# Visits of two chunks from chunk 8, seven tiles of transposed keys and queries, and new rows of operations, in a retention and squared-ReLU kernel

## The chip, the cores and the metric

One core of a Trainium2 chip. The metric is the device time of one execution in microseconds (us), median of the runs shown.

## The reference, cut to what matters

```python
# retention: q, k, v are (4, 8, 768, 64); gamma = 1 - 2**(-5 - h) for head h
for t in range(S):
    state = gamma * state + einsum('bhd,bhe->bhde', k[:, :, t], v[:, :, t])
    y[:, :, t] = scale * einsum('bhd,bhde->bhe', q[:, :, t], state)
x = y.transpose(0, 2, 1, 3).reshape(3072, 512)
h = maximum(x @ w_in, 0)          # w_in 512 x 2048
out = (h * h) @ w_out             # w_out 2048 x 512
```

## The kernel before, in words

The 3072 tokens are 24 chunks of 128, six for each of four sequences. Work is recorded as named operations, and for each engine a row of names (`TURNS`, L280 to L344) fixes by hand in which order that engine takes them. Every engine is in order: an operation that waits holds up all that stand behind it in its row. SP's row holds nearly all DMAs, ACT's some stores.

The names, with the number of a chunk or a block behind them:

- `ldq`, `ldk`, `ldv` (L694): loads of one chunk of q, k, v, 256 KB each, from SP, into one of four slots each. Chunks 0 to 3 are loaded in pairs (L529). `ldwin`, `ldwout` (L946): loads of the weights into the staging tiles `wst`; a `ldwout` and the last two `ldwin` are 1 MB.
- `cq`, `ck`, `cv`, `cwin`, `cwout`: casts of what was loaded to bf16 (L510 to L514, L704), each a quarter of a weight piece or one chunk.
- `X` (L736): the DMA transpose of the cast keys and queries of a chunk from 7 on into one of `NQT` tiles `qkT`. Chunks 4 and 5 are transposed by TensorE (`T`, `E`), chunk 6 inside visit V.5 (`E6`).
- `V m.n` (`visit`, L801): TensorE's work of a visit. It ends chunk m (values, and queries times states, into `yy`) and begins chunk n (scores and sums of keys and values, into `sc`). `U`/`V m-m.n-n` (`visit2`, L865) does that for two chunks at a time, its sums in two PSUM banks of the shared four. `P`, `S`, `Y` on VectorE mask the scores, add up the state, and scale the output into `xt`.
- `F1.b.f` (`ffn1`, L971): eight matmuls of block b of tokens with w_in; `R` (ReLU, ACT, L978) and `Q` (square, ACT or VectorE, L990 and L992) follow, through two tiles `r`.
- `F2` (L1149): the second product for chunks 0 to 3, in quarters of w_out, with `O` on ACT. `M1` to `M7` (`products`, L1079): for every later pair of chunks the second product as seven products in place of eight, with sums of weights `WT`, sums of activations `H`, and the evictions `e`, `u`, `v`, `ca`, `cb`, `cc`, `cd`.
- `st`: stores of the output.

Which form a visit has is decided by this loop (`DOUBLE` is 10, `SPLIT` is 6, `NPAIR` is 2):

```python
if n >= DOUBLE:
    if n % 2 == 0:
        visit2([x for x in (n - 2, n - 1) if n > DOUBLE or x == n - 1], [x for x in (n, n + 1) if x < NM])
elif n < 2 * NPAIR:
    ...
else:
    visit(m, n if n < NM else None, t)
```

So the visits of before are V.4, V4., V.5, V5.6, V6.7, V7.8, V8.9, V9.10-11, V10-11.12-13 and so on to V22-23. TensorE's row mixes them with groups F1, F2 and M of about 0.87 us each. A class `Plan` gives the operations their PSUM banks and tiles and puts all rows in one sequence.

Of the kernel before, what the change touches and what calls it, by code (L numbers as in the profile page):

```python
# [18 lines left out]
class Plan:  # L19
# [47 lines left out]
    def schedule(self, nbanks, max_open, nslots):  # L67
# [176 lines left out]
BLOCKS = [2, 2, 1, 1, 2, 2, 2, 2, 2, 2, 2, 2, 2]  # L244
SPLIT = 6
AHEAD = 4
DOUBLE = 10
WARM = 20.0
FILL = 0.215
WARMING = 18.4  # L250
# [28 lines left out]

TURNS = {  # L280
    "POOL": (
        "iota3 ident iota iota2 cmask2 cmask ck0.0 cq0.1 cv0.0 cv0.1 ck2.1 cv2.0 cwin1.0 cwin1.2 cq4 cwin3.2 "
        "cwin4.1 cwin5.2 cwin5.0 cwout0.3 cwout0.2 cwout1.1 cwout1.2 cwout1.3 cwout2.0 cq6 cq5 cwout3.3 cwout3.2 "
        "cq7 ck8 cq8 ck10 cq11 ck11 v.4 v.6 cq13 ck14 cq19 ck16 cq16 cq17 ck17 ck18 cq20 ck20 ck21 ck23 v.12 v.16 "
        "v.18 v.20 "
    ),
    "DVE": (
        "lng lnt ex2_f ex_f vf2 vf Ek0.0 Ek0.1 Eq0.0 P0.10 P0.01 P0.00 P0.11 S1 cq2.1 Y0.0 Y0.1 Ek2.1 P2.01 P2.00 "
        "cv2.1 cwin0.2 P2.10 S2 P2.11 cwin2.0 Y2.0 S3 Y2.1 Q0.2 cwin3.0 Eq4 cwin4.3 ck4 Q1.0 cv4 Q1.2 Ek4 Q1.10 "
        "S4.0 P4 cwin5.1 Y4 Q0.10 ck5 Q0.14 S4.1 cwout0.1 cwout1.0 WT1.0 WT1.1 cwout2.3 WT3.0 Q1.12 WT2.0 WT2.1 "  # L290
# [12 lines left out]
    "ACT": (
        "vf20 vf0 yf0 yf1 yf2 yf3 ck0.1 cq0.0 Eq0.1 cq2.0 S0 Eq2.0 ck2.0 Ek2.0 Eq2.1 cwin0.0 R0.0 cwin2.2 Q0.0 "
        "R0.2 R0.4 Q0.4 R1.0 R1.4 Q1.4 cwin4.0 cwin4.2 R1.2 R0.6 Q0.6 R1.10 R1.6 cwin5.3 Q1.6 R0.8 Q0.8 R1.8 "
        "R0.10 cwout0.0 Q1.8 R0.14 R2.4 Q2.4 R0.12 R2.12 Q0.12 R2.8 Q2.8 cwout2.2 R1.12 cwout2.1 Q2.12 R2.0 Eq5 "
        "cwout3.1 cwout3.0 Ek5 ck6 R1.14 Q2.0 O0 E6 O1 R3.8 O3 O2 R3.0 cq10 Q3.0 Q3.8 R3.12 R3.4 Q3.4 R4.4 Q4.4 "
        "R4.12 Q4.12 R4.10 R4.0 Q4.0 Q4.10 R4.6 e.4 R4.8 Q4.8 Q4.6 R4.2 Q4.2 R4.14 Q4.14 ca.4 ck12 e.6 R5.10 "
        "R5.14 cq12 R5.0 R5.4 Q5.4 R5.2 st4.0 Q5.2 R5.8 R5.6 ca.6 Q5.8 R5.12 Q5.12 st4.1 e.8 st6.1 ca.8 R6.0 R6.8 "
        "Q6.0 Q6.8 R6.4 R6.10 Q6.10 R6.12 R6.2 Q6.2 R6.6 R6.14 R7.4 Q7.4 R7.12 R7.2 Q7.2 R7.14 Q7.14 R7.6 R7.10 "  # L310
        "Q7.10 e.10 R7.0 Q7.0 st8.0 R7.8 Q7.8 Q7.6 ca.10 R8.0 R8.8 Q8.0 R8.6 Q8.8 R8.14 Q8.6 R8.10 R8.2 Q8.10 "
        "R8.4 Q8.4 R8.12 Q8.12 st10.1 e.12 R9.0 R9.2 cq21 R9.8 Q9.2 R9.4 Q9.4 st10.0 ca.12 R9.10 R9.12 Q9.8 ck22 "
        "R9.6 st12.1 R9.14 Q9.6 e.14 Q9.14 cq23 R10.8 Q10.8 R10.10 R10.6 R10.0 ca.14 R10.4 Q10.0 R10.14 Q10.14 "
        "R10.2 R10.12 Q10.2 R11.12 e.16 R11.4 R11.8 Q11.8 R11.6 R11.2 R11.10 Q11.10 R11.0 R11.14 Q11.14 ca.16 "
# [12 lines left out]
        "Tk0.0 Tk0.1 Tq0.1 Tq0.0 A0.1 A0.0 B0 B1 Tq2.0 C0.0 C0.1 Tk2.0 Tk2.1 Tq2.1 A2.0 A2.1 B2 B3 F1.0.0 C2.0 "
        "C2.1 F1.0.2 F1.0.4 F1.1.0 F1.1.4 Tq4 F1.1.2 F1.0.6 F1.1.6 Tk4 F1.1.10 F1.0.10 V.4 F1.0.8 F1.1.8 V4. "
        "F1.0.12 F1.0.14 F1.2.4 F1.2.12 F1.2.0 F1.2.8 F1.1.12 F2.1.0 F2.0.0 F2.0.1 F2.1.1 Tq5 F2.1.2 Tk5 F1.1.14 "
        "F2.0.2 F2.1.3 F2.0.3 V.5 F2.2.0 F2.2.1 F2.3.0 F2.3.1 V5.6 F2.2.2 F2.3.2 F2.3.3 F1.3.8 V6.7 F2.2.3 M1.4 "  # L330
        "F1.3.0 F1.3.12 V7.8 F1.3.4 F1.4.4 F1.4.10 F1.4.12 F1.4.0 M5.4 F1.4.6 F1.4.8 F1.4.2 M6.4 V8.9 F1.4.14 "
        "M2.4 M3.4 M7.4 M1.6 M5.6 M4.4 U9.10-11 V9.10-11 M2.6 F1.5.10 F1.5.14 F1.5.0 F1.5.4 F1.5.2 F1.5.8 M6.6 "
        "F1.5.6 M3.6 F1.5.12 M7.6 M1.8 M4.6 M5.8 U10-11.12-13 V10-11.12-13 M2.8 M6.8 M3.8 F1.6.0 F1.6.8 M7.8 "
        "F1.6.4 F1.6.10 U12-13.14-15 V12-13.14-15 M4.8 F1.6.12 F1.6.2 F1.6.6 F1.6.14 F1.7.4 F1.7.14 F1.7.12 "
        "F1.7.2 F1.7.6 M1.10 F1.7.10 M5.10 F1.7.0 U14-15.16-17 V14-15.16-17 F1.7.8 M2.10 M3.10 F1.8.0 F1.8.8 "
        "M6.10 F1.8.6 F1.8.14 M7.10 F1.8.10 F1.8.2 M4.10 F1.8.4 U16-17.18-19 V16-17.18-19 F1.8.12 M1.12 M5.12 "
        "F1.9.0 F1.9.2 F1.9.8 F1.9.4 M2.12 M6.12 M3.12 F1.9.10 M7.12 F1.9.12 F1.9.6 M4.12 U18-19.20-21 "
        "V18-19.20-21 F1.9.14 M1.14 M5.14 M6.14 F1.10.8 F1.10.10 M2.14 F1.10.6 M3.14 F1.10.0 F1.10.4 M7.14 "
        "F1.10.14 U20-21.22-23 V20-21.22-23 F1.10.2 M4.14 F1.10.12 M1.16 F1.11.12 F1.11.4 M5.16 F1.11.8 M6.16 "
        "V22-23. F1.11.6 M2.16 F1.11.2 F1.11.10 M7.16 F1.11.0 F1.11.14 M3.16 F1.12.2 M4.16 F1.12.8 F1.12.6 "  # L340
        "F1.12.10 F1.12.4 F1.12.0 F1.12.12 M1.18 M5.18 F1.12.14 M6.18 M2.18 M3.18 M7.18 M1.20 M5.20 M4.18 M6.20 "
        "M2.20 M3.20 M7.20 M1.22 M5.22 M4.20 M6.22 M2.22 M7.22 M3.22 M4.22 "
    ),
}  # L344

# [2 lines left out]
def kernel(  # L348
# [29 lines left out]
    blk0 = [sum(blocks[:i]) for i in range(NB)]  # L378
    for x, n in zip(blk0, blocks):
        assert 512 % (n * C) == 0 and x // 4 == (x + n - 1) // 4  # L380
    NLD, NBF, NQT, NXT, NH2, NWS, NOSB, NST = 4, 5, 5, 3, 3, 4, 3, 6
    NR, NUN = 2, 2
    NBANK = 4

# [3 lines left out]
    def sb(name, shape, dt):  # L388
        return const.tile(shape, dt, name=name)

    ident = sb("ident", [P, P], BF16)
    cmask = sb("cmask", [P, L], BF16)
# [12 lines left out]
    cmask2 = sb("cmask2", [P, 2, C], BF16)  # L405
# [773 lines left out]
    for m in range(-1, NM):  # L1179
        n = m + 1  # L1180
        if n > DOUBLE:
            xs = range(prepared, min(NM, n + AHEAD) if n % 2 else prepared)
# [6 lines left out]
        t = m + 2 if NPE <= m + 2 < NTD else None  # L1189
# [65 lines left out]
```

## Time and profile before

| | us |
|---|---|
| runs, median of 3 (lowest to highest) | 207.31 (206.76 to 207.9) |
| profiled execution, its own time | 207.57 |
| its span, first to last instruction | 205.8 |
| busy: PE, DVE, ACT, POOL | 192.9, 144.5, 121.1, 37.3 |
| HBM read, written | 27.26 MB, 6.29 MB |

Busy times come from one profiled execution, whose own time stands 0.26 us above the median. PE is TensorE's matmuls, PEld its weight loads, DVE VectorE, POOL GpSimd, SP the engine whose queue issues DMAs. In the timeline of an engine, square brackets tell of idle time before an instruction and of what ended it. The chain of waits is followed back from the last instruction; "issue" is a wait for nothing that the profile shows. Matmul ends are modelled and overlap, so steps from start to start are used for PE. The landing of a load is the time at which its semaphore is complete, issue plus time to landing in the view of the DMA issues.

### The profile page before, as it was taken

The numbers are of one execution on the slowest core, as the hardware profiler recorded it, in microseconds if no ns is written. First come the engines' busy times: TensorE is split into PE (matmuls) and PEld (weight loads), VectorE is DVE, ScalarE is ACT, GpSimd is POOL, SyncE is SP. The second block draws the span as 40 slices with busy tenths as digits, with TensorE's granted clock in tenths as the row PEclk, the third lists the DMA queues.
The fourth block names the chain that finished last, engine by engine and source line by source line (L and its number), as shares of the span: only waits on it lengthen the run. The fifth ranks groups of instructions, "written<-read, shape, count | busy, mean of one in ns | idle before, by whom it ended". The sixth has DMA issues, their size and how long they took to land.

```text
span 205.8 us, 7031 instructions
## 1 busy us (share of the span) xinstructions
PE 192.9 (94%) x3030; PEld 160.7 (78%) x3034; DVE 144.5 (70%) x287; ACT 121.1 (59%) x216; POOL 37.3 (18%) x62
## 2 busy tenths in 40 slices
PE   8988999969799999998899999989999999999993
PEld 6655888744479788887788898878888988888882
DVE  2586687554764978869778978796778797576332
ACT  8463699679037992771357977666575555764110
POOL 6532314451300132001114012113000020001100
PEclk9996999999999999999999999999999999999999
DMA  5999999999999999999999999999961100020222
GB/s 163 290 317 320 291 316 358 300 272 204 217 205 250 172 243 160 231 234 250 182 187 204 147 268 189 221 227 195 160 171 58 45 12 3 27 76 3 104 102 102
DMA packets 95503, 38.46 MB, mean 187 GB/s; under 512 B 81008, under 2 KB 89456, under 8 KB 95472
## 3 DMA queue, kind: packets, MB, share of 16 engines
q1 hardware_dynamic: 93744, 35.00, 81.2%
q10 hardware_dynamic: 1728, 3.02, 4.3%
q8 instruction: 23, 0.38, 0.8%
q14 instruction: 8, 0.07, 0.1%
HBM read 27.26 MB, written 6.29 MB: 163 GB/s over the span
## 4 chain that ended last, share of the span: by engine, by line
PE 59%; DMA 18%; SPq 16%; POOL 2%; issue 2%; DVE 1%; ACT 1%; ACTq 0%; POOLq 0%
PE fps L971 28%; PE fps L1079 27%; DMA kn<-in_k_dram 8%; SPq L694 7%; SPq L946 5%; DMA wst<-in_moe_w_out_dram 5%; DMA qkT<-kqs 5%; SPq L529 2%; SPq L736 2%; PE sc L786 1%; POOL w_out L514 1%; PE yy L760 1%; PE yy L775 1%; PE fps L798 1%; DVE h L992 1%
## 5 line engine op out<-in xcount | busy, mean ns | idle before, releaser
L971 PE MATMUL fps<-xt,w_in 128*128 128x256 bf16 (+1 forms) x832 | 92.3, 266 | 0.9 <-ACT w_in L510 0.5
L971 PEld LDWEIGHTS <-w_in 128*128 128x128 bf16 x832 | 75.5, 98 | 9.9 <-ACT w_in L510 0.6
L978 ACT ACTIVATE r<-fps 128x512 f32<-128x512 f32 x96 | 55.8, 592 | 41.6 <-PE fps L971 37.1
L990 ACT ACTIVATE h<-r 128x512 bf16<-128x512 f32 x60 | 37.1, 626 | 1.1
L1079 PEld LDWEIGHTS <-h 128*128 128x128 bf16 x320 | 31.0, 98 | 5.7 <-issue 1.8
L992 DVE TENSOR_TENSOR h<-r 128x512 bf16<-128x512 f32 x36 | 26.2, 732 | 8.6 <-ACT r L978 8.1
L1079 PEld LDWEIGHTS <-wst 128*128 128x128 bf16 x240 | 23.5, 98 | 3.8 <-issue 1.0
L1079 PE MATMUL fps<-w_out,h 128*128 128x256 bf16 x160 | 20.9, 273 | 0.7 <-issue 0.7
L1079 PE MATMUL fps<-wst,h 128*128 128x256 bf16 x160 | 20.7, 273 | 0.6 <-DVE wu L1102 0.6
L1079 PE MATMUL fps<-wst,wst 128*128 128x256 bf16 x160 | 20.6, 272 | 0.0
L514 POOL CAST kqs<-kn 128x512 bf16<-128x512 f32 x10 | 7.2, 718 | 47.3 <-DMA kn<-in_k_dram 23.5
L704 DVE TENSOR_TENSOR vs<-vn,vf 128x512 bf16<-128x512 f32 x20 | 13.6, 686 | 3.0 <-DMA vn<-in_v_dram 3.0
L1149 PE MATMUL fps<-w_out,h 128*128 128x512 bf16 x60 | 14.2, 379 | 0.5 <-issue 0.5
L514 POOL CAST kqs<-qn 128x512 bf16<-128x512 f32 x11 | 7.8, 706 | 26.8 <-DMA qn<-in_q_dram 11.5
L1105 ACT ACTIVATE wst<-fps 128x512 f32<-128x512 f32 x10 | 5.9, 592 | 10.9 <-PE fps L1079 10.9
L919 DVE TENSOR_TENSOR state<-fps,state 128x256 bf16<-128x256 f32 x23 | 9.7, 420 | 3.2 <-PE yy L775 2.7
L1113 ACT ACTIVATE osb<-fps 128x256 f32<-128x256 f32 x10 | 3.8, 381 | 13.6 <-PE fps L1079 13.5
L927 DVE TENSOR_TENSOR xt<-yy,yf 128x512 bf16<-128x512 f32 x15 | 10.0, 682 | 2.3 <-PE yy L775 2.3
L1079 PE MATMUL fps<-w_out,wst 128*128 128x256 bf16 x80 | 10.5, 272 | 0.8 <-issue 0.8
L1149 PEld LDWEIGHTS <-h 128*128 128x128 bf16 x64 | 6.0, 98 | 6.4 <-issue 0.2
L1102 DVE TENSOR_TENSOR osb<-fps,wst 128x256 f32<-128x256 f32 x15 | 6.3, 420 | 6.2 <-PE fps L1079 2.9
L775 PE MATMUL yy<-qkT,state 64*64 64x64 bf16 x296 | 8.4, 195 | 1.1 <-DVE state L851 1.0
(99 smaller groups left out, 208.7 us busy)
## 6 DMA issues: line engine op xcount, KB each, us to landing
qn<-in_q_dram SPq DMA_DIRECT2D x20, 256.0 KB, 5.5
kn<-in_k_dram SPq DMA_DIRECT2D x20, 256.0 KB, 5.5
vn<-in_v_dram SPq DMA_DIRECT2D x20, 256.0 KB, 5.8
wst<-in_moe_w_out_dram SPq DMA_DIRECT2D x4, 1024.0 KB, 9.7
out_dram<-osb SPq DMA_DIRECT2D x10, 256.0 KB, 4.3
out_dram<-osb ACTq DMA_DIRECT2D x9, 256.0 KB, 3.1
wst<-in_moe_w_in_dram SPq DMA_DIRECT2D x4, 512.0 KB, 8.5
wst<-in_moe_w_in_dram SPq DMA_DIRECT2D x2, 1024.0 KB, 8.5
```

Source lines behind the costliest of these rows:

```text
L514: nc.gpsimd.tensor_copy(o, t)
L694: lambda x=x, t=t: nc.sync.dma_start(t.rearrange("s (h d) -> s h d", h=H), src[x][b, :, i * C : (i + 1) * C, :].rearrange("h s d -> s h d")))
L704: lambda: nc.vector.tensor_tensor(out=o[:], in0=t.rearrange("s (h d) -> s h d", h=H), in1=vf[:, i, :, None].to_broadcast([P, H, D]), op=AL ...
L775: nc.tensor.matmul(yy[L * c : L * c + L, sub, 256 * x + p * L : 256 * x + p * L + L], lhsT=st[r, j, :], rhs=qkT[r, 1, j, sub * L : sub * L ...
L927: lambda xt=xt, u=u, i=i, x=x: nc.vector.tensor_tensor(out=xt[:, :, u * C : u * C + C].rearrange("s p (g t) -> s g p t", g=2), in0=yy[:, : ...
L946: lambda: nc.sync.dma_start(st, wv))
L971: nc.tensor.matmul(ps[:, u * n : u * n + n], lhsT=w_in_bf[j][:, cb, c * P : (c + 1) * P], rhs=xt[:, cb, cols], start=(cb == 0), stop=(cb = ...
L978: nc.scalar.activation(o, t, AF.Relu)
L990: nc.scalar.activation(hv, rv, AF.Square)
L992: (nc.vector if on == "DVE" else nc.gpsimd).tensor_tensor(out=hv, in0=rv, in1=rv, op=ALU.mult)
L1079: nc.tensor.matmul(ps[:, 256 * half : 256 * half + 256], lhsT=a[left][:, f], rhs=right(f), start=(first and f == 0), stop=True, skip_group ...
L1149: nc.tensor.matmul(ps[:, 0:w], lhsT=h2[:, fb, u * C : u * C + C], rhs=w_out_bf[j][:, c, ns], start=(fb == 0), stop=(fb == NFB - 1))
```

## The change

`DOUBLE` goes from 10 to 8, so chunks 8 and 9 are begun and ended in visits of two: V7.8-9, V8-9.10-11, V10-11.12-13 in place of V7.8, V8.9, V9.10-11, V10-11.12-13. `NQT` goes from 5 to 7 tiles `qkT`. The rows of all five engines are other ones, with the same operations; some move to another engine (casts, squares, stores).

```diff
-DOUBLE = 10
+DOUBLE = 8
...
-    NLD, NBF, NQT, NXT, NH2, NWS, NOSB, NST = 4, 5, 5, 3, 3, 4, 3, 6
+    NLD, NBF, NQT, NXT, NH2, NWS, NOSB, NST = 4, 5, 7, 3, 3, 4, 3, 6
```

SP's row up to X15, then TensorE's row up to V10-11.12-13, before and after (the rows run on in the same manner):

```diff
-ldk0 ldq0 ldv0 ldq2 ldk2 ldv2 ldwin0 ldwin1 ldwin2 ldq4 ldwin3 ldwin4 ldk4 ldv4 ldwin5 ldwout0 ldk5
-ldwout1 ldwout2 ldq6 ldq5 ldwout3 ldk6 ldv5 ldk7 ldq7 ldv6 ldk8 ldq8 ldv7 X7 ldv8 st0 ldq10 X8 ldq9 ldk9
-ldv9 ldk10 st3 st2 ldk11 ldq11 X9 ldv10 ldv11 X10 ldk12 X11 ldq13 ldv12 st1 ldq12 ldq14 ldk13 ldv13
-ldk15 ldq15 ldk14 X12 X13 ldq19 ldv14 X14 ldv15 X15
+ldk0 ldq0 ldv0 ldq2 ldk2 ldv2 ldwin0 ldwin1 ldwin2 ldq4 ldwin3 ldwin4 ldk4 ldv4 ldwout0 ldq5 ldq6 ldwin5
+ldv5 ldk5 ldwout1 ldq7 ldk6 ldwout3 ldwout2 ldk7 ldv6 ldk9 ldq9 ldk8 ldq8 ldv7 X7 ldv9 ldv8 X9 X8 st0
+ldq11 ldk12 ldq10 ldk10 ldk11 ldv10 ldq13 st2 st3 ldq12 ldv11 X10 ldk13 X11 st1 X12 ldv12 ldv13 X13
+ldq15 ldq14 ldk15 ldk14 st6.0 ldq17 ldv14 ldv15 X15 ldv16 X14
...
-Tk0.0 Tk0.1 Tq0.1 Tq0.0 A0.1 A0.0 B0 B1 Tq2.0 C0.0 C0.1 Tk2.0 Tk2.1 Tq2.1 A2.0 A2.1 B2 B3 F1.0.0 C2.0
-C2.1 F1.0.2 F1.0.4 F1.1.0 F1.1.4 Tq4 F1.1.2 F1.0.6 F1.1.6 Tk4 F1.1.10 F1.0.10 V.4 F1.0.8 F1.1.8 V4.
-F1.0.12 F1.0.14 F1.2.4 F1.2.12 F1.2.0 F1.2.8 F1.1.12 F2.1.0 F2.0.0 F2.0.1 F2.1.1 Tq5 F2.1.2 Tk5 F1.1.14
-F2.0.2 F2.1.3 F2.0.3 V.5 F2.2.0 F2.2.1 F2.3.0 F2.3.1 V5.6 F2.2.2 F2.3.2 F2.3.3 F1.3.8 V6.7 F2.2.3 M1.4
-F1.3.0 F1.3.12 V7.8 F1.3.4 F1.4.4 F1.4.10 F1.4.12 F1.4.0 M5.4 F1.4.6 F1.4.8 F1.4.2 M6.4 V8.9 F1.4.14
-M2.4 M3.4 M7.4 M1.6 M5.6 M4.4 U9.10-11 V9.10-11 M2.6 F1.5.10 F1.5.14 F1.5.0 F1.5.4 F1.5.2 F1.5.8 M6.6
-F1.5.6 M3.6 F1.5.12 M7.6 M1.8 M4.6 M5.8 U10-11.12-13 V10-11.12-13
+Tk0.0 Tk0.1 Tq0.1 Tq0.0 A0.1 A0.0 B0 B1 Tq2.0 C0.0 C0.1 Tk2.0 Tk2.1 Tq2.1 A2.0 A2.1 F1.0.0 B2 F1.0.2 B3
+C2.0 C2.1 Tq4 F1.0.4 F1.1.4 F1.1.2 F1.1.6 F1.1.0 Tk4 F1.0.6 V.4 F1.1.8 F1.1.10 V4. F1.0.10 F1.0.8 F1.2.0
+F1.2.4 F1.2.8 Tq5 F1.0.12 F1.1.14 F1.0.14 F1.2.12 F1.1.12 Tk5 F2.0.0 F2.1.0 V.5 F2.1.1 F2.0.1 F2.0.2
+F2.0.3 F2.1.2 F2.2.0 F2.1.3 V5.6 F2.2.1 F2.2.2 F1.3.4 F1.3.12 F1.3.0 V6.7 F2.2.3 F2.3.0 F2.3.1 F2.3.2
+F2.3.3 U7.8-9 V7.8-9 F1.3.8 F1.4.4 F1.4.12 F1.4.10 F1.4.6 M1.4 F1.4.2 F1.4.0 M5.4 F1.4.14 F1.4.8 M6.4
+M2.4 M3.4 M7.4 M1.6 M5.6 M4.4 U8-9.10-11 V8-9.10-11 M2.6 M6.6 M3.6 F1.5.2 F1.5.12 F1.5.14 M7.6 F1.5.0
+U10-11.12-13 V10-11.12-13
```

ACT's row of after has, around the casts of w_out, `cwout1.3 Q0.14 cwout3.3 cwout2.1 cwout2.2 cwout3.0 ck7 R1.12 Q2.12 E6 O0`. SP's row between X15 and X19 gains, ahead of X17, the loads ldq18 and ldv18, and ahead of X18 the loads ldk20, ldk21, ldq21 and ldq22.

## The prediction

> **What bounds the kernel now.** I read the page, then the busy times by window, the waits and timeline of PE, and the chain of waits. The page first:
>
> ```profile
> PE 192.9 (94%) x3030; PEld 160.7 (78%) x3034; DVE 144.5 (70%) x287; ACT 121.1 (59%) x216; POOL 37.3 (18%) x62
> DMA  5999999999999999999999999999961100020222
> q1 hardware_dynamic: 93744, 35.00, 81.2%
> ```
>
> PE is busy for 94% of the span, yet the 16 DMA engines are full too, from the start to slice 29, about 150 us. Nearly all of it is one queue, SP's, and what stands late in SP's row lands late. By window (us, PE, PEld, DVE, ACT, POOL, granted clock, DMA share, GB/s):
>
> ```profile
> 15.00:20.00 5.00, 3.85 (x64) 2.29 (x62) 3.46 (x8) 1.23 (x3) 1.17 (x2) 0.74 1.14 319
> 20.00:25.00 5.00, 4.85 (x69) 4.15 (x66) 2.99 (x6) 3.35 (x7) 1.23 (x2) 0.91 1.15 325
> 40.00:45.00 5.00, 3.37 (x19) 1.51 (x18) 3.10 (x5) 3.33 (x6) 2.34 (x3) 1.00 0.86 244
> 95.00:100.00 5.00, 3.95 (x152) 3.38 (x152) 4.97 (x12) 0.60 (x1) 0.00 (x0) 1.00 1.23 144
> 170.00:175.00 5.00, 5.00 (x48) 4.47 (x47) 3.77 (x8) 2.95 (x5) 0.00 (x0) 1.00 0.01 3
> ```
>
> PE has holes at 40 to 45 and 95 to 100, and none near the end. The timeline of PE says what ended the larger ones:
>
> ```profile
> 43.98 0.40 PE L745 MATMUL fps<-ident,kqs 128*128 128x128 bf16 x4 [1.63 <-POOL kqs L514]
> 54.42 0.25 PE L775 MATMUL yy<-qkT,state 64*64 64x64 bf16 x6 [0.97 <-DVE state L851]
> 93.13 1.03 PE L1079 MATMUL fps<-wst,h 128*128 128x256 bf16 x8 [0.62 <-DVE wu L1102]
> 99.73 0.49 PE L1079 MATMUL fps<-w_out,wst 128*128 128x256 bf16 x3 [0.85 <-issue]
> ```
>
> The first is Tq5 behind cq5 behind ldq5, a load that stands late in SP's row. The chain of waits shows the same queue further on:
>
> ```profile
> 27.07 10.15 DMA wst<-in_moe_w_out_dram
> 49.09 4.68 DMA kn<-in_k_dram
> 91.98 3.85 DMA qkT<-kqs
> 99.41 5.94 DMA qkT<-kqs
> 105.39 0.32 PE sc L786 x16
> ```
>
> The transposes X13 and X15 land at 95.83 and 105.35, and the scores of their visits start 0.04 us later. After 105.4 the chain is almost PE alone. So up to about 105 us the SP queue is level with PE, and afterwards PE sets the end.
>
> **The change part by part.** *Visits.* V7.8, V8.9, V9.10-11 and V10-11.12-13 become V7.8-9, V8-9.10-11 and V10-11.12-13. From start to next start the undisturbed ones before took 0.66 and 0.73 (one chunk each way) and 1.16 to 1.22 us (two). V7.8-9 and V9.10-11 lie between; I take 1.0. The sum goes from 0.66+0.73+1.0+1.2 to 1.0+1.2+1.2: 0.2 to 0.3 us of PE saved.
>
> *Seven tiles.* They let a transpose land before the visit that reads its predecessor is over. Before, the X transposes wait for casts or simply queue: X15 reuses chunk 10's tile, which is free at 96.6, and is issued at 99.41 behind ldv15. So more tiles release nothing that waits; worth 0, except that pairs at chunk 8 would need them.
>
> *New rows: which loads come when.* This decides. Cost per entry from landings before (issue plus time to landing): from ldv4 (27.35) to ldwout3 (45.88) five 1 MB weights and three 256 KB loads took 18.53; to ldv7 (55.92) eight loads took 10.04, that is 1.25 each; to X11 (80.38) eleven loads, three stores and about 4.5 transposes took 24.46. With stores 0.75 (most of their steps are 0.69 to 0.76) and a load 1.2 this gives 2.0 for a transpose, half of it behind its landing, and 3.0 for a weight. Undisturbed loads step by 1.05, undisturbed weights by 2.87; these are the lower bounds.
>
> (a) Weights. Up to ldv4 SP's row is the same. Then ldwout2 comes last of the weights, behind five weights (its own included) and six loads in place of three: 27.35+5x3.0+6x1.2 = 49.5 (48.0 at the lower bounds; before, the last weight landed at 45.88). ACT casts two of its quarters one after the other, 0.63 each: ready at 50.8. PE gets to F2.0.2, which reads it, much sooner. In the new row F1.0.0 still starts near 17.5; then come B2, F1.0.2, B3, C2.0, C2.1 and Tq4, so F1.0.4 starts about 22.95 (before 22.10, without Tq4). Five F1 groups at 0.874 to 27.3, Tk4, F1.0.6 and V.4 to 28.9, two groups and V4. to 31.3, five groups and Tq5 to 35.9, one us for ldwin5's casts, five groups to 41.3, Tk5, two F2 groups of 0.87, V.5 (0.66), two more F2: 45.7. PE then stands for 5 us; nothing else in its row may pass.
>
> (b) After it: five F2 groups to 55.1, V5.6 (0.8) to 55.9, five groups to 60.3, V6.7 to 61.0, five to 65.4. V7.8-9 wants X8 and X9. Counting from before's X9 (73.20), four loads and three stores are no longer ahead of X8, the later one: 73.20-4.8-2.3 = 66.1; counted forward from ldwout2 it is 65.3. I take 65.7, the visit ends at 66.4. Before, V5.6 was through at 55.17 with 150 matmul groups (F1, F2, M) left; now 55.9 with 153. That is 3.3 us behind.
>
> (c) Eighteen groups (15.7) bring PE to 82.2. X11 has three more loads ahead: 80.38+3.6 = 84.0, or 83.5 counted forward. V8-9.10-11 ends at 84.4, 0.7 after X11, as V10-11.12-13 and V12-13.14-15 did after X13 and X15. X13 has four loads fewer ahead, 91.0, and does not hold V10-11.12-13 (91.8). Fourteen groups later V12-13.14-15 meets X14 at 105.5 to 106.6 (before X15 105.35; two loads and a store more, a load and a store fewer) and ends at 106.7.
>
> (d) Fifteen groups: 119.9. X17 has two loads more ahead: 118.86+2.4 = 121.2, or 120.7. V14-15.16-17 ends at 121.7 with 88 groups left. Before it ended at 119.57, also with 88 left. X18, with four loads more and a store fewer ahead, lands at 133.2, when PE comes to V16-17.18-19; X21 (146.5) is early, and from there the same 75 groups follow. Behind by 121.7-119.6 = 2.1 us.
>
> *Code fetch.* 6079 PE instructions are fetched in 23 packets (the instruction queue of the page). The two stalls put down to issue, 1.01 at M3.8 and 0.92 at M1.12, both stand 256 instructions behind a point 37 or 20 instructions into a visit of two chunks. In the new row such points lie 8 into V8-9.10-11 and 23 into V16-17.18-19; the others lie deeper. Two again, and the first runs while X11 is awaited. Taken as nothing; bounds -0.9 and +0.9.
>
> *Clock.* The two windows at 15 to 25 lose 0.26x5+0.09x5 = 1.75 us of clock after a thin stretch of PE; the 1.63 us hole at 42 lost none (1.00). The 5 us hole lies beyond that, so its price is between 0 and 1.75. I take 0 at the end: PE's row by itself ends V14-15.16-17 at 120.2 (the no-change rival), and 1.75 more is 121.95, within 0.3 of where X17 puts it anyway. The Trainium skill (TensorE: Matmul & The Clock Gate, "What's actually happening") says that the clock falls to half after an idle window of about 3.4 us; by that rule the new hole does cost the clock, and the sum would be 0.2 us more, 209.6. The start of this trace agrees with a drop to half and back.
>
> *Moved casts and squares.* Six squares go from DVE to ACT (6x0.63 on ACT, which is busy 59%), three casts of w_out from POOL to DVE and ACT, one v from DVE to POOL. ACT is fullest at 60 to 80 (15.1 of 20 us), where PE waits for X11 anyway: that wait of 1.5 us hides it. Without that cover it costs up to the 0.56 us that F1.4.12 waited before.
>
> **Sum.** The profiled execution before took 207.57 (span 205.8 and 1.8 around it), 0.26 over the median of 207.31. 207.31+2.1 = 209.4.
>
> **Rivals.** *Faster: the loads come in time.* If loads cost 1.05, weights 2.87 and transposes 1.9 throughout, ldwout2 lands at 48.0, F2.0.2 starts at 49.3, and X8, X11, X14 and X17 land at 62.2, 78.8, 99.2 and 112.2, ahead of PE. PE's row then reaches the end of V14-15.16-17 at 118.7, 0.9 ahead of before, and one code stall less makes 1.8: 205.5. It decides from X17 before 119 and F2.0.2 before 50. For it: the quick steps are the common ones. Against it: the same queue took 1.2 to 1.25 on average in every long stretch.
>
> *No change: only the weight is late.* F2.0.2 at 50.8 as forecast, but X11 to X17 in time. PE's own row then ends V14-15.16-17 at 120.2, 0.65 late: 208.0.
>
> *Much slower.* X18 needs 1.6 us more than counted because ACT's stores share the engines (134.8), and the late code stall follows: 2.1+0.6+0.9 gives 210.9, and another 0.9 with a stall at V8-9.10-11 uncovered: 211.8.
>
> *The tiles do nothing.* If something waited for tiles that I missed, X15 would land earlier than its place in the row says; at most its wait of 0.3 us.
>
> **How the numbers follow.** Forecast 0.58, much slower 0.10, no change 0.16, faster 0.16. 0.5% is 1.04 us, about what a measurement of this kernel can tell. The range goes from 206.6 (the faster case without the code stall, 206.4, all but taken in) to 211.8; what is left out is most of the faster case. Its own range for the forecast is 208.4 to 210.4. Faster 0.16, same 0.16, slower 0.68.
>
> **What would show it.** Right: a PE hole of 4 to 6 us before an L1149 group near 46 to 51, ended by a cast of w_out; V14-15.16-17 starting its scores as X17 lands near 121; no other hole above 1 us after 135. Wrong: the w_out hole under 3 us, or the scores of chunks 14 to 17 starting without a wait for qkT; then PE's row alone decides, and it is the no-change or faster case.

## The result, and the profile after

After took 214.64 us (median; 213.92 to 216.57), the runs of before beside it 207.03: a ratio of 1.0376, 95% interval 1.0294 to 1.0458. Ratios here and below leave out the runs that fell in a slower state of the chip and are not taken from the medians, so the two differ a little. The forecast was 209.4 with a range from 206.6 to 211.8. The direction was right, and 5.2 us were missing from the sum. The profiled execution took 215.31 with a span of 213.5, 7.7 us above that of before. The page after:

```profile
PE 193.3 (91%) x3029; PEld 159.8 (75%) x3033; DVE 140.8 (66%) x282; ACT 124.2 (58%) x224; POOL 35.2 (16%) x59
PEclk9999999997699999999999999999999999999999
DMA  6999999999999999999999999999702100011222
q1 hardware_dynamic: 93888, 35.27, 80.2%
```

PE is busy 0.4 us longer than before; the rest of the 7.7 stands as idle time, though part of the busy time ran at a lower clock. The DMA engines are full for the same 150 us. New is the dent in the granted clock, in slices 10 and 11. By window (us, PE, PEld, DVE, ACT, POOL, granted clock, DMA share, GB/s):

```profile
15.00:20.00 5.00, 2.90 (x35) 1.84 (x34) 2.78 (x6) 1.80 (x4) 1.68 (x4) 1.00 1.15 320
20.00:25.00 5.00, 4.80 (x98) 3.98 (x97) 4.01 (x6) 2.89 (x5) 2.83 (x4) 1.00 1.14 325
...
45.00:50.00 5.00, 1.88 (x27) 0.89 (x15) 1.12 (x2) 0.63 (x1) 0.89 (x2) 1.00 1.09 358
50.00:55.00 5.00, 3.00 (x8) 1.05 (x8) 3.74 (x7) 3.95 (x7) 1.39 (x2) 0.56 0.90 186
55.00:60.00 5.00, 4.84 (x79) 2.20 (x79) 0.12 (x1) 1.78 (x4) 1.82 (x3) 0.76 1.24 211
```

From 45 to 50 PE is idle for 3 us; from 50 to 60 it is busy, but at 0.56 and 0.76 of its clock. The timeline of PE has the largest holes from 40 us on, with their releasers in brackets:

```profile
52.00 7.12 PE L1148 MATMUL fps<-w_out,h 128*128 128x512 bf16 x20 [4.96 <-POOL w_out L513]
...
90.01 0.39 PE L1078 MATMUL fps<-wst,wst 128*128 128x256 bf16 x2 [1.00 <-issue]
...
136.00 1.03 PE L970 MATMUL fps<-xt,w_in 128*128 128x256 bf16 x8 [1.54 <-ACT r L977]
...
142.28 0.49 PE L1078 MATMUL fps<-wst,wst 128*128 128x256 bf16 x3 [0.74 <-issue]
```

The first is the hole before F2.0.2 that was forecast. The 20 matmuls behind it take 7.12 us; in a kernel shown below, at full clock, the same 20 take 4.49. The third was not forecast. What held ACT's R8.8 is seen in ACT's timeline:

```profile
130.26 0.60 ACT L977 ACTIVATE r<-fps 128x512 f32<-128x512 f32 x1 [0.43 <-PE fps L970]
134.92 0.34 ACTq L1123 DMA_DIRECT2D out_dram<-osb  x1
135.36 0.60 ACT L977 ACTIVATE r<-fps 128x512 f32<-128x512 f32 x1 [4.50 <-DVE h L1053]
```

Between R8.2 and R8.8 stands the issue of a store, st10.0, which before stood fourteen operations further on in ACT's row. Its data were ready at 132.16 (cb.10), yet it is issued at 134.92. The transpose X19 landed at 134.84, and in three other kernels with this row the store was issued 0.08 us after X19 landed as well (132.71 after 132.64, 136.03 after 135.95, 133.71 after 133.63). So the store waited for an unrelated transfer. The traces show by what: right ahead of this store ACT waits for a DMA semaphore, number 104 in all four kernels, and X19 reports its landing by this same semaphore, as the store itself does later. The releaser in brackets (DVE h) is only what came last by the profile's account.

The chain of waits, early part:

```profile
27.15 8.80 DMA wst<-in_moe_w_in_dram
41.43 9.60 DMA wst<-in_moe_w_out_dram
51.08 0.88 POOL w_out L513
52.00 7.12 PE fps L1148 x20
```

Before, the chain ran through loads of keys and the transposes X13 and X15 up to 105 us. Now it goes through ldwin5 and the last weight, which lands at 51, and is on PE from there, but for the store near 131.

Where the 7.7 us lie can be counted on PE's row: start-to-start time less 0.874 us for each group and the undisturbed steps of the visits (0.70, 0.95 and 1.17). What is left is lost time:

| stretch of PE's row | lost before, us | lost after, us |
|---|---|---|
| F1.0.4 to V5.6 | 2.2 | 11.1 |
| V5.6 to V10-11.12-13 | 3.1 | 1.6 |
| V10-11.12-13 to V14-15.16-17 | 1.8 | 0.3 |
| V14-15.16-17 to V16-17.18-19 | 0.2 | 2.5 |
| from there to the end | 1.2 | 1.2 |

The sum is 8.3 more. Against it stand the three visits, which step by 0.35 us less than the four of before, Tq4, which after has behind it at F1.0.4 (0.24), and a start of F1.0.4 at 22.00 in place of 22.10; that leaves 7.6 of the 7.7. In the first row 4.96 of after's 11.1 are the hole and 2.7 the slower clock behind it; another 1.39 are a wait of F1.0.12 at 37.65, where the prediction had one us for the casts of ldwin5.

### The profile page after: what moved, and what is told of

It reads as the page before. It is cut to its first block, busy times and chain, and to the rows that moved or that the text cites. A ratio compares the mean times of both kernels' runs of the same rounds, so it can differ in the third digit from the quotient of the medians.

```text
span 213.5 us, 7037 instructions
## 1 busy us (share of the span) xinstructions
PE 193.3 (91%) x3029; PEld 159.8 (75%) x3033; DVE 140.8 (66%) x282; ACT 124.2 (58%) x224; POOL 35.2 (16%) x59
## 4 chain that ended last, share of the span: by engine, by line
PE 55%; DMA 23%; SPq 9%; DVE 5%; issue 3%; POOL 2%; ACT 2%; POOLq 0%; DVEq 0%; ACTq 0%
PE fps L1078 23%; PE fps L970 21%; DMA wst<-in_moe_w_in_dram 9%; DMA kn<-in_k_dram 7%; PE fps L1148 6%; DMA wst<-in_moe_w_out_dram 4%; SPq L693 4%; DMA vn<-in_v_dram 3%; SPq L735 2%; SPq L528 2%; PE yy L759 1%; ACT r L977 1%; PE yy L774 1%; DVE pt L904 1%; PE sc L785 1%
## 5 line engine op out<-in xcount | busy, mean ns | idle before, releaser
L970 PE MATMUL fps<-xt,w_in 128*128 128x256 bf16 (+1 forms) x832 | 90.5, 264 | 4.5 <-ACT r L977 2.9
L989 ACT ACTIVATE h<-r 128x512 bf16<-128x512 f32 x66 | 40.1, 625 | 0.9
L991 DVE TENSOR_TENSOR h<-r 128x512 bf16<-128x512 f32 x30 | 21.6, 724 | 7.1 <-ACT r L977 6.8
L1148 PE MATMUL fps<-w_out,h 128*128 128x512 bf16 x60 | 16.6, 431 | 5.5 <-POOL w_out L513 5.0
L703 DVE TENSOR_TENSOR vs<-vn,vf 128x512 bf16<-128x512 f32 x20 | 14.4, 730 | 3.6 <-DMA vn<-in_v_dram 3.6
L513 POOL CAST kqs<-qn 128x512 bf16<-128x512 f32 x9 | 6.0, 671 | 59.5 <-DMA qn<-in_q_dram 59.5
L918 DVE TENSOR_TENSOR state<-fps,state 128x256 bf16<-128x256 f32 x27 | 11.4, 421 | 3.5 <-PE yy L774 2.7
L926 DVE TENSOR_TENSOR xt<-yy,yf 128x512 bf16<-128x512 f32 x17 | 11.4, 683 | 2.6 <-PE yy L774 2.6
L1108 POOL TENSOR_TENSOR wu<-wst 128x256 f32<-128x256 f32 x4 | 2.9, 731 | 53.5 <-DVE wst L1053 38.6
L904 DVE TENSOR_TENSOR pt<-sc,cmask 128x512 bf16<-128x512 f32 x16 | 10.9, 682 | 0.0
```

The source lines that it names most:

```text
L513: nc.gpsimd.tensor_copy(o, t)
L703: lambda: nc.vector.tensor_tensor(out=o[:], in0=t.rearrange("s (h d) -> s h d", h=H), in1=vf[:, i, :, None].to_broadcast([P, H, D]), op=AL ...
L904: lambda pt=pt, x=x: nc.vector.tensor_tensor(out=pt[:], in0=sc[:, :, 256 * x : 256 * x + 256].rearrange("s g (p t) -> s g p t", p=NJ), in1 ...
L918: nc.vector.tensor_tensor(out=sts[j1][:], in0=cc, in1=sts[j0][:], op=ALU.add)
L926: lambda xt=xt, u=u, i=i, x=x: nc.vector.tensor_tensor(out=xt[:, :, u * C : u * C + C].rearrange("s p (g t) -> s g p t", g=2), in0=yy[:, : ...
L970: nc.tensor.matmul(ps[:, u * n : u * n + n], lhsT=w_in_bf[j][:, cb, c * P : (c + 1) * P], rhs=xt[:, cb, cols], start=(cb == 0), stop=(cb = ...
```

## The experiments

Median and ratio are beside the runs of before in the same job. "Lost" is counted as in the table.

**e1_fill.** The hole at F2.0.2 filled with 128 small matmuls:

```diff
+ if o["name"] == "F2.0.2": 128 x matmul(fps[spare][0:64, 0:64], lhsT=ident[:, 0:64], rhs=ident[:, 0:64])
```

> The kernel after, with 128 small matmuls of the identity (64x64, into the PSUM bank that F2.2.0 opens next) put ahead of F2.0.2, where TensorE stood idle from 46.7 to 52.0 us. 128 matmuls with their weight loads are 256 instructions, so that all later work keeps its place in the blocks in which code is fetched. Theory cold clock: the granted clock was 0.5 from 50.57 for 6.83 us, of which 5.4 us were under work, so 2.7 us were lost; with the idle time filled the half-clock stretch is gone and the run is 2.2 to 2.7 us faster, near 212.1. Rival, the late weight alone: the same groups wait for the same cast, the time is that of after within 0.4 (214.6). Rival, the filler is longer than the wait: F2.0.2 starts later than 52.0 by what it is too long.

212.89 us, 1.0228 (1.0170 to 1.0286), 1.75 below after. Its timeline of PE:

```profile
48.24 2.91 PE L1225 MATMUL fps<-ident 128*64 128x64 bf16 x86
52.46 1.49 PE L1225 MATMUL fps<-ident 128*64 128x64 bf16 x42 [1.31 <-issue]
53.88 4.49 PE L1148 MATMUL fps<-w_out,h 128*128 128x512 bf16 x20
```

The filling ran too long, so F2.0.2 started 1.9 us later than in after; even so V5.6 came 0.75 earlier. From F2.0.2 to V5.6 0.05 us are lost in place of 2.68. So the clock is a cost of its own, on top of the wait. Not all of the 1.75 us comes from here: the stall at M6.6 (1.2 us of lost time in after) was absent in this execution.

**e2_st10.** The store from ACT's row to SP's:

```diff
-ACT: ... R8.2 st10.0 R8.8 ...
+ACT: ... R8.2 R8.8 ...      SP: ... X19 X18 st10.0 ldk23 ...
```

> The kernel after, with the store st10.0 moved from ACT's row to SP's, behind X18. In after ACT stood from 130.85 to 134.86 at st10.0, whose wait is on a DMA semaphore that X19 completed at 134.84, and R8.8 behind it held up TensorE for 1.54 us at 136.0. Theory store: that stall goes, 1.5 us faster, near 213.1, ACT has no gap over 2 us there. Rival, the SP queue (X18 lands at 135.9, just ahead of V16-17.18-19 at 138.7): with the stall gone TensorE comes to that visit at 137.2, still after X18, so nothing is given back. Rival, slot or VectorE: R8.8 waits for Q8.2 at 135.83 on VectorE, and the time stays at 214.6.

211.32 us, 1.0145 (1.0067 to 1.0223). From V14-15.16-17 to V16-17.18-19 0.83 us are lost in place of 2.55; the stall at M6.6 was absent in this execution too. Of the 3.3 us the store accounts for 1.7 directly; 1.5 in all were expected. Behind F2.0.2 half clock lasted 3.41 us in place of 6.83, which is another 0.95.

**e3_early_before and e4_early_after.** The rows of before up to V6.7 with the rows of after from V7.8-9 on; and the rows of after up to F2.3.3 and X7 with the rows of before from V7.8 on.

> Rows of before up to V6.7, X7 and what they need, rows of after from V7.8-9 on (DOUBLE 8, seven tiles); at the seam F1.3.8 to F1.3.4 with their R, Q and O keep the order of before, st0 stands ahead of X9, and cq9 behind O2. Theory early rows: the loss of after lies ahead of V5.6 (7.4 us behind at equal work there); with the early rows of before the time falls to 207 to 208.5. Theory SP queue: TensorE now comes 6 us earlier to the later visits, whose transposes land where the row has them (X11 82.7, X14 108.2, X17 123.7, X18 135.9 in after), so V14-15.16-17 ends near 124.4 in place of 119.6 and the time is 210.5 to 212. Theory visits of two: the late rows cost what after costs, 213 to 215.

> The mirror image: rows of after up to F2.3.3 and X7, rows of before from V7.8 on (DOUBLE 10, five tiles); at the seam F1.3.8 stands ahead of M1.4 and the R, Q and O of block 3 are in the order of TensorE. Theory early rows: about 7 us behind at the seam, of which the holes of before that waited for loads (0.56, 0.78, 0.35, 0.2) give back up to 1.9: 212 to 214.5. Theory SP queue or visits of two as the main cost: most of the loss is in the late rows, and the time is 207 to 210.

e4: 213.19 us, 1.0226 (1.0153 to 1.0300). The early rows alone cost some 5 us: a hole of 3.15 before F2.0.2 and half clock from 49.75 to 53.17. e3: 216.54 us, 1.0420 (1.0354 to 1.0486), but it does not price the late rows, since at the seam I had put cq9 behind O2 in ACT's row. That held X9 in SP's row for 4.7 us, and X8 behind it, and V7.8-9 waited 3.36 for X8. e3b_seam mends this.

**e3b_seam.** As e3, with cq9 on POOL, X8 ahead of X9 in SP's row (`X7 ldk9 st0 ldq9 X8 ldv8 ldv9 X9`), and st10.0 on SP.

> Rows of before up to V6.7, rows of after from V7.8-9 on, with chunk 9's loads and casts placed so that X9 is not held, and st10.0 issued by SP. Theory A (the loss is the late weight with its half clock, and ACT's store): without the early rows and the store nothing is left but a wait of about 1.2 us at V7.8-9, whose X9 should land near 65.5; 207.4 to 209.0 beside 207.5 for before, and V14-15.16-17 does not wait for X17. Theory B (SP's queue sets the end in the late rows): X17 lands near 121 to 122, V14-15.16-17 starts its scores as it lands, and the time is 209.6 or more. Theory C (the pairs at chunk 8 cost by themselves): chunk 9 is wanted about ten us earlier than before, and V7.8-9 waits more than 3 us for X9: 210.5 or more.

211.13 us, 1.0135 (1.0062 to 1.0207): the time of theory C, with a wait of 2.28 us where it had more than 3. PE at V7.8-9:

```profile
66.86 0.37 PE L786 MATMUL sc<-qkT 64*64 64x64 bf16 x16 [2.28 <-DMA qkT<-kqs]
...
68.58 6.64 PE L971 MATMUL fps<-xt,w_in 128*128 128x256 bf16 x36 [0.80 <-DVE xt L927]
```

and by window:

```profile
67.50:70.00 2.50, 1.70 (x30) 1.19 (x20) 2.03 (x5) 0.00 (x0) 0.62 (x1) 0.50 1.37 222
70.00:72.50 2.50, 2.50 (x14) 1.76 (x12) 2.02 (x3) 1.51 (x3) 1.91 (x2) 0.50 1.06 183
```

X9 landed at 66.82 and PE was there at 64.1. 6.2 us are lost at this place: the wait, the wait for Y7 behind it, and half clock for 6.8 us. From V8-9.10-11 on the late rows lose only 2.2 us, where those of before lose 4.3 from V8.9 on; V14-15.16-17 did not wait for X17. So with this order of loads a pair at chunk 8 wants chunk 9 sooner than the full DMA queue brings it; in after PE is late enough not to notice, and in e17 below, with the order of after, the two are level.

**e5b_ldq7_st10.** e2 with one load moved:

```diff
-SP: ldwout1 ldq7 ldk6 ldwout3 ldwout2 ldk7
+SP: ldwout1 ldk6 ldwout3 ldwout2 ldq7 ldk7
```

> The rows of after with st10.0 on SP, and ldq7 moved from ahead of ldwout3 to behind ldwout2, so that one load of 256 KB less stands ahead of the last weight. Theory A: the weight lands about 1.2 us earlier (49.8 in place of 51.0), the hole at F2.0.2 shrinks from 5.0 to about 3.8, and the time is 1.0 to 1.6 under that of the kernel with the store alone moved (211.3): 209.7 to 210.3. If the hole is then too short to cost the clock, another 1.5 goes. Rival (what is gained early is given back at X11 or X17): still 211.

213.11 us, 1.0241 (1.0196 to 1.0286), slower than e2. The weight did land sooner, at 48.08 in place of 51.03, which is more than the 1.2 us that were expected, but DVE's row has cq7 ahead of Ek5:

```profile
41.69 0.85 DVE L511 CAST w_out<-wst 128x512 bf16<-128x512 f32 x1 [0.40 <-DMA wst<-in_moe_w_out_dram]
49.23 0.43 DVE L511 CAST kqs<-qn 128x512 bf16<-128x512 f32 x1 [6.69 <-DMA qn<-in_q_dram]
49.57 0.42 DVE L511 COPY qkT<-fps 128x512 bf16<-128x512 bf16 x1
```

The cast waits 6.69 us for the load that I delayed, and Ek5, which V.5 reads, waits behind it. PE then stands 5.4 us at V.5 instead. So the edit spoiled the run, and its time does not price the load.

**e6_tiles.** The kernel before with seven tiles.

```diff
-    NLD, NBF, NQT, NXT, NH2, NWS, NOSB, NST = 4, 5, 5, 3, 3, 4, 3, 6
+    NLD, NBF, NQT, NXT, NH2, NWS, NOSB, NST = 4, 5, 7, 3, 3, 4, 3, 6
```

> The kernel before with seven tiles of transposed keys and queries in place of five, nothing else. My forecast: nothing waits for a tile, so the same time within 0.4 us, and X15 lands near 105.3 as before. Rival: a transpose did wait for a tile that the trace did not show; X15 then lands earlier by the wait and the time falls by 0.5 or more.

207.87 beside 207.89: 0.9998 (0.9963 to 1.0033). X15 landed at 106.58, so no earlier than in before (105.35). The tiles do nothing by themselves.

**e9_shift.** After, with every filling matmul of the start split in two:

```diff
-for _ in range(o.get("fill", 0)): matmul(fps[bank][:, 0:2 * P], ident, ident twice)
+for _ in range(2 * o.get("fill", 0)): matmul(fps[bank][:, 0:P], ident, ident)
```

> The kernel after, with each of its 37 filling matmuls of the first 16 us split into two of half the width: 74 more PE instructions ahead of everything else, the same work. Theory: the stalls of about 1 us behind V8-9.10-11 (M6.6) and V16-17.18-19 (M5.12) come from fetching code, and belong to the place of the block boundaries; shifted by 74 instructions no boundary falls near the start of a visit of two, both stalls are gone, and the time is 0.9 to 2.1 under after: 212.5 to 213.7. Rival: they are waits for something that the profile does not show and stay where they are: the time of after, 214.6.

213.96 us, 1.0289 (1.0227 to 1.0351), 0.7 below after and just short of the gain that was expected. Both stalls are gone: over V8-9.10-11 with the groups up to V10-11.12-13 0.26 us are lost in place of 1.30, and from V16-17.18-19 to V18-19.20-21 0.12 in place of 1.06. The store's hole happened to be longer and took some of it back:

```profile
134.79 1.86 PE L970 MATMUL fps<-xt,w_in 128*128 128x256 bf16 x8 [2.69 <-ACT r L977]
```

Eight matmuls take 1.86 behind it, 1.03 in after: this hole cost the clock too.

**e13_mended and e14_mended_fill.** e5b with cq7 behind cwout2.3 and the split fills; then ten more filling matmuls ahead of F2.0.2.

> After with four places mended: st10.0 on SP, ldq7 behind ldwout2, its cast cq7 behind cwout2.3 in DVE's row (in e5b_ldq7_st10 cq7 stood ahead of Ek5 and held V.5), and the 37 filling matmuls split so that no block boundary of the code falls into a visit of two. Theory A (early weight, clock, store and code stalls are the whole loss, and the late SP queue follows PE): last weight at 48 to 48.7, hole at F2.0.2 about 2.5, no stall at M6.6, M5.12 or R8.8: 206.3 to 208.2, where the half clock decides within that. Theory B (SP's queue binds as soon as PE is earlier): V8-9.10-11 waits for X11 (82 to 83), V14-15.16-17 for X17 (121 or later): 209.5 to 211.

> The same with ten filling matmuls (256 columns of ident, some 2.2 us) in PE's row ahead of F2.0.2, where PE would stand idle for the weight. Theory: the clock is not lowered behind the hole; if it was in e13_mended, 1.5 to 2 us less than that run, otherwise the same within 0.5. Rival (the half clock has nothing to do with the idle time): half clock all the same.

e13: 211.42 us, 1.0162 (1.0115 to 1.0208). e14: 209.63 us, 1.0053 (1.0018 to 1.0089). Neither theory of e13 gave the number. The weight landed at 49.8, not 48; the hole was 3.41 with 6.8 us of half clock behind it. X11 landed at 85.02, 0.4 us before V8-9.10-11 came to its scores (85.43), and V14-15.16-17 came 1.2 us after X17: level, but not waiting. e14's filling left 2.11 us idle, and half clock came for 3.4 us in place of 6.8. Its time is 1.8 below e13, as expected, though the clock was still lowered once.

**e7_before_sp and e10_sp_shift.** The kernel before with loads moved in SP's row; then with the code shifted by 120 instructions.

```diff
-SP: ... ldwout2 ldq6 ldq5 ... ldv13 ldk15 ldq15 ldk14 X12 X13 ldq19 ldv14 ... X17 ldq18
+SP: ... ldwout2 ldq5 ldq6 ... ldv13 X12 X13 ldk15 ldq15 ldk14 ldv14 ... X17 ldq19 ldq18
```

> The kernel before with SP's row changed: ldq5 ahead of ldq6 (and cq5 ahead of cq6), X12 and X13 ahead of ldk15, ldq15 and ldk14, and ldq19 (with its cast) behind X17 in place of ahead of X14. Theory (before 105 us SP's queue and PE are level): the hole at Tq5 falls from 1.6 to about 0.5, X13 lands near 92 and X15 near 104.2, and 0.8 to 1.3 us of that reaches the end: 206.2 to 207.0 beside 207.6. Rival (PE finds its next wait at once): the same time.

> As e7_before_sp, with 60 more PE instructions pairs ahead of everything (the fills split, 28 more of the smallest warming matmuls, 3 fills fewer), so that no code block's boundary falls into or just ahead of a visit of two. Theory of the code stalls: those at M3.8 and M1.12 (1.0 and 0.9) go, the time is 1.0 to 1.9 under e7_before_sp: 204.5 to 205.8. Rival: the time of e7_before_sp.

e7: 211.91 us, 1.0138 (1.0067 to 1.0210); e10: 212.11, 1.0195 (1.0150 to 1.0240). X13 landed at 93.02 and the hole at Tq5 fell to 0.94, about as expected, but DVE's row has cq15 ahead of cd.6 and H1.8, and ldq15 now came at 96.31. DVE, and then PE, in e7:

```profile
96.34 0.43 DVE L512 CAST kqs<-qn 128x512 bf16<-128x512 f32 x1 [4.15 <-DMA qn<-in_q_dram]
96.68 0.42 DVE L1102 TENSOR_TENSOR wu<-fps,wu 128x256 f32<-128x256 f32 x1
```

```profile
97.15 1.62 PE L1079 MATMUL fps<-wst,h 128*128 128x256 bf16 x8 [3.90 <-DVE wu L1102]
```

The same trap as in e5b. e10's shift, expected to gain 1.0 to 1.9 us, gained nothing that the times show: from V16-17.18-19 to V18-19.20-21 0.13 us are lost in place of 0.54, but half clock behind the hole lasted 6.83 us in place of 3.41.

**e17_f2 and e18_f2_fill.** e13 with real work in the hole; then also with work ahead of V7.8-9.

```diff
-PE: F2.0.1 F2.0.2 F2.0.3 F2.1.2 F2.2.0 F2.1.3 V5.6 F2.2.1 F2.2.2
+PE: F2.0.1 F2.2.0 F2.2.1 F2.0.2 F2.1.2 F2.0.3 F2.1.3 V5.6 F2.2.2
-NQT 7, NOSB 3, pl.schedule(NBANK, 2, NR)
+NQT 6, NOSB 4, pl.schedule(NBANK, 3, NR)
 e18 only:
-PE: F2.3.3 U7.8-9 V7.8-9 F1.3.8 ... M1.4
+PE: F2.3.3 F1.3.8 M1.4 U7.8-9 V7.8-9 ...
```

> As e13_mended, and in PE's row F2.2.0 and F2.2.1 (which need no late weight) stand ahead of F2.0.2, and F2.1.2 ahead of F2.0.3; four tiles osb in place of three, so that O3 need not wait for st0, paid for with six tiles qkT. 1.7 us of the wait for the last weight are filled with work. Theory A (hole and clock are the early loss): the hole falls to 1.5 to 2 us, the clock is not lowered there, and the time falls by up to 3.4 against e14_mended_fill (209.6): 206.2 to 207.5. Theory C (the pairs at chunk 8 want X8 and X9 at once, and the late weight only hides it): V7.8-9 then comes to its scores near 64 and waits 2 to 3 us for X8 (66.3), perhaps with half clock behind it: 208.3 to 209.8.

> As e17_f2, with F1.3.8 and M1.4 moved from behind V7.8-9 to ahead of it, 1.7 us of work for that wait. Theory C: the wait at V7.8-9 falls to 0.5 to 1.5 us, and the time is 1.0 to 1.7 under e17_f2: near 207. Theory A: nothing to win there, the time of e17_f2.

e17: 209.51 us, 1.0036 (0.9992 to 1.0080); e18: 209.82, 1.0060 (1.0023 to 1.0096). e17's timeline of PE:

```profile
45.50 3.40 PE L1148 MATMUL fps<-w_out,h 128*128 128x512 bf16 x15 [0.16 <-issue]
50.00 3.61 PE L1148 MATMUL fps<-w_out,h 128*128 128x512 bf16 x16 [1.09 <-POOL w_out L513]
...
60.18 0.32 PE L785 MATMUL sc<-qkT 64*64 64x64 bf16 x16 [1.59 <-DVE state L850]
```

The hole is 1.09, the clock stays full, and from F1.0.4 to V5.6 3.5 us are lost, against 11.1 in after and 8.4 in e14. Yet the time is that of e14: from V5.6 to the end 6.0 us are lost in place of 3.1, 1.6 of them in a wait of V6.7 for DVE's state, 1.4 between V7.8-9 and V8-9.10-11. X8 landed at 65.47 as V7.8-9 came to its scores at 65.52, so e18's work there won nothing. Theory C gave the time of e17, but not the place: the wait of 2 to 3 us for X8 did not come, and 1.59 stand at V6.7 instead. What is gained early is mostly given back to waits that stood close behind.

**e12_before_shift and e15_before_rows.** The kernel before with its code shifted by 120 instructions; then also with ldq5 ahead of ldq6, ldk14 behind X13, and ldq19 with its cast behind X17.

```diff
-for _ in range(PRE): matmul(fps[NBANK - 1][0:1, 0:1], one, one)
+for _ in range(PRE + 28): matmul(fps[NBANK - 1][0:1, 0:1], one, one)
 (and the fills split as in e9_shift, three fewer)
```

> The kernel before with 60 more pairs of PE instructions ahead of all its work (the fills split, 28 more of the smallest warming matmuls, 3 fills fewer); rows unchanged. Theory of the code stalls: M3.8 and M1.12 (1.0 and 0.9) lose their stalls; the first is covered by the wait for X15, the second reaches the end: 206.2 to 207.2 beside 207.7. Rival: the time of before.

> As e12_before_shift, with ldq5 ahead of ldq6 (cq5 ahead of cq6), ldk14 behind X13, and ldq19 with its cast behind X17. In e7_before_sp the loads ldq15 and ldk15 had been moved too, and cq15, which stands in DVE's row ahead of cd.6 and H1.8, held both (a hole of 3.9 us); here no cast that moves has urgent work behind it. Theory (SP's queue and PE level up to 105 us): hole at Tq5 about 0.5, X15 near 104.3, 1 to 1.5 us under e12_before_shift: 205.0 to 206.0. Rival: the same time as e12_before_shift.

e12: 207.00 beside 208.04 us, 0.9942 (0.9911 to 0.9972). e15: 206.84, 0.9917 (0.9885 to 0.9949). Both beat before, by 0.6% and 0.8%; between the two the intervals tell nothing apart. So e12's theory held, and e15's forecast of another 1 to 1.5 us failed: its rival, the time of e12, came. In e12 V16-17.18-19 to V18-19.20-21 loses 0.13 in place of 1.05 us. In e15 the hole at Tq5 (2.08 in e12) is gone, and V7.8's scores wait for X8:

```profile
65.17 0.32 PE L786 MATMUL sc<-qkT 64*64 64x64 bf16 x16 [1.34 <-DMA qkT<-kqs]
```

## Why the prediction was right and wrong

**Visits and tiles: right.** The three visits step by 0.95, 1.17 and 1.20, the four of before by 0.66, 0.73, 1.08 and, where undisturbed, 1.2: 0.35 us saved, 0.2 to 0.3 forecast. Seven tiles do nothing (e6).

**(a) The weight: right in kind, 1.2 us short.** The hole of 5 us came as forecast (4.96), ended by a cast of w_out. But the weight landed at 51.0, not 49.5, and F2.0.2 started at 52.0, not 50.8. That the hole kept its size is luck, since PE had arrived 1.3 us later as well (47.0, not 45.7). The price per load and weight missed something in SP's row: the issue of ldwout3 took 3.14 us (38.19 to 41.33), against 0.49 in e5b, and ldwout2 could only be issued behind it, at 41.43 against 38.17. What held that issue is not settled.

**Clock: the step that failed.** I took 0 within bounds of 0 to 1.75, because X17 would set the end of V14-15.16-17 anyway. Five F2 groups from 52.00 to 59.05 took 7.05 us and not 4.37: 2.7 lost. With the 1.2 above this makes 7.2; V5.6 was 7.4 us behind at equal work and not 3.3. The bound itself was too low: it came from the start of the trace of before, where half clock lasted 3.41 us, and behind the new hole it lasted 6.83, of which 5.4 had work. The rule of the Trainium skill that I had weighed (TensorE: Matmul & The Clock Gate, "What's actually happening") was the better guide, as the clock did fall behind the new hole. This trace agrees with it in its 6.83 us at half clock, twice the 3.41 of before.

**(c) and (d), SP's queue sets X11, X14 and X17: wrong as a bound.** X11 landed at 82.7 (83.5 to 84.0 forecast), X14 at 108.2 (105.5 to 106.6 forecast), X17 at 123.7 (121.2 forecast), and none of them held PE, though X17 came only 0.3 us before the scores that read it: V14-15.16-17 began its values at 123.63 and stepped on after the undisturbed 1.17. The sums treated the queue as a clock of its own. With the rows of after, or nearly these, it moves with PE: X17 landed at 123.7, 122.2, 120.7 and 119.8 in after, e13, e14 and e17, where V10-11.12-13 had ended at 96.8, 94.5, 93.1 and 93.0. In e3b, with other rows ahead, X17 came 23.7 us behind that end and not some 27, so PE is not all that sets it; how the two are tied is not shown. That X17 covers the clock's loss is in any case no argument: it lands later where PE is later. What was right is that part of the early loss is given back: 7.4 us behind at V5.6 became 5.2 at the end of V14-15.16-17 (119.57 before, 124.81 after). Of the 1.8 us that before loses between V10-11.12-13 and V14-15.16-17, 0.6 are the waits of its visits for X13 and X15, and 1.0 is the stall at M3.8; after loses 0.3 there, and had its own such stall at M6.6, further ahead.

**Moved operations: a term left out.** I priced casts and squares, and not the store that ACT issues 0.1 us ahead of a ReLU that PE wants. It held ACT for 4 us and PE for 1.5; with the waits next to it, 2.4 us more are lost in that stretch than before. That makes 5.2 into 7.7. "No other hole above 1 us after 135" was the sign that failed.

**Code fetch: right places, wrong cover.** The stalls stood behind V8-9.10-11 and V16-17.18-19 (1.00 and 0.74 of idle time). The first was to be hidden by X11, which held nothing. As before had two as well, the sum of 0 stands for this execution; the first stall was absent in e1, e2 and e3, whose code lies in the same places there.

**Rivals.** "Much slower" named X18 as the mechanism; X18 landed 2.8 us before PE came. "Faster" needed the weight before 50. "No change" had the mechanism that came nearest, PE's own row with X11 to X17 in time: its 208.0, with 1.2 for the weight, 2.7 for the clock and 2.4 for the store, makes 214.3. That the weight's wait alone is not the end of it is seen in e17: mended, the new rows are level with before, not better. And e17 has the shifted code, which before has not; beside the shifted e12 of the same job (207.00, 0.9942) it is slower by about 1%, and the two intervals do not meet.

## What to carry to other kernels

When a change makes a busy engine wait for more than some 2 us, price the wait and the slower clock behind it as two terms, and cover neither with a transfer whose place in the queue depends on that same engine. When a load moves later in an in-order queue, look up its cast, and move that too: e5b, e7 and e10 lost 3.9 to 5.4 us in a hole behind a cast that waited ahead of urgent work. A store on a compute engine's row is a wait for everything behind it, and it can wait for a transfer that it has nothing to do with, when the two share a semaphore.

## What was unexpected of the hardware

The clock, by hole. Each row gives PE's idle time in one hole behind the start of the run, and the stretch at half clock that follows it in the trace:

| hole, us (kernel) | half clock behind it, us |
|---|---|
| 5.4 (e5b), 4.96 (after), 4.57 (e9), 3.95 (e10), 3.41 (e13) | 6.83 |
| 3.90 (e7), 3.36 (e3), 3.35 (e2), 3.15 (e4), 2.69 (e9) | 3.41 |
| 2.28 (e3b) | 6.83 |
| 2.23 (e6), 2.19 (e3b), 2.13 (e1), 2.05 (e2), 1.99 (e14) | 0 |
| 2.11 (e14), 2.08 (e12), 2.02 (e3) | 3.41 |
| 1.78 (e18), 1.63 (before), 1.31 (e1), 1.09 (e17) | 0 |

All stretches are 3.41 or twice that. Above 2.6 us every hole listed cost the clock, below 1.8 none. In between the length of the hole does not decide, but its place does. In each trace all changes of the clock lie a whole number of times 3.41 us apart, so they mark windows that run by themselves. Two holes of like length, e6's of 2.23 and e12's of 2.08, by these windows (e6's are counted back from its only change, at 207.10; columns as above):

```profile
39.85:43.26 3.41, 2.17 (x10) 0.68 (x7) 1.60 (x3) 1.86 (x4) 2.21 (x4) 1.00 0.76 157
43.26:46.68 3.42, 2.33 (x21) 1.73 (x22) 2.17 (x3) 1.91 (x4) 1.28 (x2) 1.00 1.11 336
```

```profile
41.99:45.40 3.41, 1.33 (x11) 0.53 (x8) 2.73 (x4) 2.78 (x6) 1.85 (x3) 1.00 1.00 299
45.40:48.81 3.41, 3.41 (x17) 2.08 (x16) 0.90 (x2) 2.54 (x6) 1.17 (x2) 0.50 1.30 245
```

e6's hole is split, 1.2 and 1.1 us idle in two windows, and the clock stays; e12's lies in one window, 2.08 us idle, and the next window has half clock. Over all 18 traces, from 35 to 195 us, half clock followed each of the 14 full-clock windows with 2.02 us idle or more (e3) and none with 1.79 or less (e2). It lasted a second window where the first one still had 0.8 us idle or more (six times, e3b's 0.80 the least), and one window where the first had 0.03 or less. The Trainium skill (TensorE: Matmul & The Clock Gate, "What's actually happening") has a window that runs by itself, and these traces agree. It puts the drop after an idle window of about 3.4 us. Here 2.02 us idle in one window were enough. At the start of a run, with its thin work, idle time alone does not tell: the stretch at half clock there was 0 (after), 3.41 (before, e2), 6.83 (e1) or 10.24 us (e15), and after, e2 and e1 have the same rows there. That moves single profiles by a us or two.

The code stalls belong to places: instructions added ahead of all work moved the code, and the stall behind V16-17.18-19 went. From there to V18-19.20-21 the ten kernels without such a shift (e1 among them, whose 256 added instructions leave the places as they are) lose 0.54 to 1.21 us, the eight with it (e9, e10, e12 to e15, e17, e18) 0.12 or 0.13. The place alone does not make a stall: the one behind V8-9.10-11 is there in after, e3b and e5b (0.7 to 1.3 lost) and absent in e1, e2 and e3 (0.12), with the code where it was. The instruction queue of the page fetches 23 packets for about 6070 instructions of PE in the trace, one for 264, if all of them are PE's. The Trainium skill (Advanced Engine Details and Errata, "ISA Cache") gives lines of 256 instructions, which is close.

What stays open: what held the issue of ldwout3, why a code stall comes in one execution and not in another, how far SP's queue is tied to PE, and whether e17 is slower than the unshifted before at all, which its interval does not tell.
